# Attention and feed-forward on one Trainium2 core: three tiles of the normalised x turned by DMA instead of by TensorE

## The chip, the core and the metric

The kernel runs on 1 core of one Trainium2 chip. The time is device microseconds (us) of one execution; where several executions are given, the median stands. The profile is one execution taken by the hardware profiler. PE is TensorE (PEld its weight loads), ACT is ScalarE, DVE is VectorE, POOL is GpSimd and SP is SyncE, which here only issues DMAs.

## The reference

```python
def _attn_ref(q, k, v, g_norm):                 # q, k, v: 8 batches, 8 heads, 576 rows, 64
    kv = np.einsum('bhsd,bhse->bhde', k, v)
    out = np.einsum('bhsd,bhde->bhse', q, kv)
    rms = np.sqrt(np.mean(out * out, axis=-1, keepdims=True) + 1e-06)
    return (out / rms * g_norm)
def _moe_ref(x, g_ln, w_ch1, w_ch2):            # x: 8, 576, 512
    mu = np.mean(x, axis=-1, keepdims=True)
    var = np.mean((x - mu) ** 2, axis=-1, keepdims=True)
    xn = (x - mu) / np.sqrt(var + 1e-06) * g_ln
    ch = np.maximum(xn @ w_ch1, 0.0) @ w_ch2    # 512 -> 2048 -> 512
    return (x + ch)
```

The attention has no softmax: k and v of a batch make one 64x64 matrix for each head, and q is multiplied with it. Its output, normalised for each head, is the x of a feed-forward part with a layer norm in front.

## The kernel before

The 8 x 576 rows of x are cut into 36 tiles of 128 rows, numbered in the order in which they are worked on; tiles 0 to 8 are of batches 0 and 1, tiles 9 to 17 of batches 2 and 3, and so on, and the last of each nine holds 64 rows of both batches. Four tiles make a block. Batch 3 begins with tile 13.

A tile's way is in `plan_tile` (L738): the attention matmul (`t_out`, L444), the squares on ACT (L457), their sums on DVE (L466), the root on ACT (L470), x on DVE (L492 or L496), its mean, and the centred and scaled `xc` in bf16 (`t_xc`, L518, three buffers). The feed-forward needs `xc` with its features in the partitions, so each tile's 128x512 is turned into `xT`, a buffer for a block. This is done in one of two ways:

- on TensorE (`t_turn_pe`, L525): four 128x128 transposes into PSUM, and a copy to `xT` on ACT (`t_turn_out`, L532);
- by DMA (`t_turn_dma`, L536): one `dma_start_transpose` on SP's queue straight from `xc` to `xT`.

The condition at L785, `n < N_PE_TURN` with 12, picks the first for tiles 0 to 11 and the second for tiles 12 to 35.

The first matmul of the feed-forward (`m1`) runs tile by tile for blocks 0 and 1 (L575) and for a whole block of four tiles from block 2, that is tiles 8 to 11, on (L590). The second (`m2`) is L609. Its result is scaled and added to x on DVE (L616) and stored from SP (L622).

The k, v and q of a batch are loaded by POOL's queue (L232, L239, L247), permuted by copies on ACT (L373), and q of batches 2 to 7 is then turned by one large DMA transpose on SP's queue into `qT` (L413); k and v make the head matrices in L421. For batches 3 to 7 POOL first waits in `gate` (L683) until the xT of a certain tile is there: tiles 5, 6 and 7 for batch 3's k, q and v, and tiles 11, 12 and 13 for batch 4's.

Nothing is scheduled by a compiler. All pieces are declared as steps with an engine, an assumed cost, a key of priority and their dependencies, and `run_plan` (L104) puts them in order: it takes the step that can start first by its assumed costs, and among equals on one engine the one with the lowest key. The DMAs go through one assumed server, one after the other. The copies of k and q of batch 3 wait in the plan for 6 us behind the planned landing of their load (`x.lag`, L716). Each engine then works through its list strictly in that order, and real waits are on semaphores. A DMA turn of a tile is planned with an occupancy of 1.235 us on SP and 0.5 us in the server; a PE turn with 0.23 us on PE and a copy of a PSUM tile on ACT.

Of the kernel before, what the change touches and what calls it, by code (L numbers as in the profile page):

```python
# [14 lines left out]
def kernel(  # L15
# [27 lines left out]
    N_TILES = B * S // 128  # L43
    N_BLK = N_TILES // 4
    FINE = (0, 1)
    N_PE_TURN = 12
    N_SUM = 12
    LOOK = 8
    XB = 18
# [44 lines left out]
    def add(eng, occ, dur, key, deps, fn, dma=None, alloc=None, main=False, lag=0.0):  # L94
        s = Step()
        s.eng, s.occ, s.dur, s.key, s.fn = eng, occ, dur, key, fn
        s.deps = [d for d in deps if d is not None]
        s.dma, s.alloc, s.main, s.frees, s.behind = dma, alloc, main, None, None
        s.start = s.done = None
        s.lag = lag  # L100
        steps.append(s)
        return s
# [335 lines left out]
    def t_out(n, h0=0, h1=H):  # L438
        bs, t = TILES[n]
        ps = psum.tile([128, H, D], f32, tag="out", name="out_ps", bufs=BANKS["out"])  # L440
        o3 = ps.rearrange("p h e -> p (h e)").rearrange("p (hp he) -> p hp he", hp=HP)
        for hp in range(h0 // 2, h1 // 2):
            for i, b in enumerate(bs):
                nc.tensor.matmul(  # L444
                    o3[:, hp, :], lhsT=att[b]["qT"][:, 4 * t + hp, :],
                    rhs=kv_pack[b % 3][:, hp, :],
                    start=(i == 0), stop=(i == len(bs) - 1))
        st[n]["ps", h0] = ps
# [6 lines left out]
    def t_sq(n, h0=0, h1=H):  # L455
        sq = buf(n, "sq", [128, H, D], h0)
        nc.scalar.activation(sq[:, h0:h1, :], st[n]["ps", h0][:, h0:h1, :], func=AF.Square)  # L457

    def t_xg(n, h0=0, h1=H):
        xg = buf(n, "xg", [128, H, D], h0)  # L460
        nc.vector.tensor_mul(xg[:, h0:h1, :], st[n]["ps", h0][:, h0:h1, :],  # L461
                             gn.to_broadcast([128, h1 - h0, D]))

    def t_red(n, h0=0, h1=H):
        ss = buf(n, "ss", [128, H, 1], h0)
        nc.vector.tensor_reduce(ss[:, h0:h1, :], st[n]["sq"][:, h0:h1, :], axis=AX.X, op=ALU.add)  # L466

    def t_rms(n, h0=0, h1=H):
        rms = buf(n, "rms", [128, H, 1], h0)
        nc.scalar.activation(rms[:, h0:h1, :], st[n]["ss"][:, h0:h1, :], func=AF.Sqrt,  # L470
                             scale=1.0 / D, bias=eps_attn)

    def t_inv(n, h0=0, h1=H):
        inv = buf(n, "inv", [128, H, 1], h0)
        nc.vector.reciprocal(inv[:, h0:h1, :], st[n]["rms"][:, h0:h1, :])
# [9 lines left out]
    def t_x(n, h0=0, h1=H):  # L485
        m, i = divmod(n, 4)
        block_tiles(m)
        x = buf(n, "x", [128, H, D], h0, XB)
        inv = st[n]["inv"][:, h0:h1, :].to_broadcast([128, h1 - h0, D])
        if n < N_SUM:  # L490
            sums = blk[m]["sums"][:, i, 0:1] if h1 == H else blk[m]["half"]
            nc.vector.tensor_tensor_reduce(  # L492
                out=x[:, h0:h1, :], in0=st[n]["xg"][:, h0:h1, :], in1=inv, scale=1.0, scalar=0.0,
                op0=ALU.mult, op1=ALU.add, accum_out=sums)
        else:
            nc.vector.tensor_mul(x, st[n]["xg"], inv)  # L496
        if h1 == H:
            st[n]["x"] = x.rearrange("p h d -> p (h d)")

    def t_mean(n):  # L500
        m, i = divmod(n, 4)
        if n < N_SUM:
            if n in HALVED:
                nc.vector.tensor_scalar(
                    blk[m]["mv"][:, i, 0:1], blk[m]["sums"][:, i, 0:1], blk[m]["half"], 1.0 / Dm,
                    op0=ALU.add, op1=ALU.mult)
            else:
                nc.vector.tensor_scalar_mul(
                    blk[m]["mv"][:, i, 0:1], blk[m]["sums"][:, i, 0:1], 1.0 / Dm)
        else:  # L510
            stats = work.tile([128, 6], f32, tag="stats", name="stats")
            nc.vector.bn_stats(stats, st[n]["x"])  # L512
            nc.vector.bn_aggr(blk[m]["mv"][:, i, :], stats)
# [15 lines left out]
    def t_turn_out(n, f0=0, f1=Dm):  # L529
        m, i = divmod(n, 4)  # L530
        kk = slice(f0 // 128, f1 // 128)
        nc.scalar.copy(blk[m]["xT"][:, kk, i * 128:(i + 1) * 128], st[n]["tps", f0][:, kk, :])  # L532
# [205 lines left out]
    def plan_tile(n):  # L738
        bs, t = TILES[n]
        m, i = divmod(n, 4)  # L740
        p = pos[n]
        dn = done[n]
        deps = []
        for b in bs:
            deps += adone[b]["kv"] + adone[b]["qT", t]
        if n >= 12:
            deps.append(main_at(okey[n] - EARLY))
        def cost(c, h0, h1):
            return c((h1 - h0) * D)
        halves = ((0, H // 2), (H // 2, H)) if n in HALVED else ((0, H),)  # L750

        q0 = okey[n] if n // 4 not in FINE else p - 12
        xs = []
        for h0, h1 in halves:
            hh = dict(h0=h0, h1=h1)
            w = (h1 - h0) / H
            d = [adone[0]["kv"][h0 // 4], adone[0]["qT", 0][h0 // 4]] if n in HALVED else deps
            o = add("PE", 0.23 * len(bs) * w, 0.23 * len(bs) * w + 0.2, okey[n], d,
                    lambda hh=hh: t_out(n, **hh), alloc="out")
            sq = add("ACT", *cost(act_cost, h0, h1), q0 + 4,  # L760
                     [o] + [done[n - 3]["red"] if n >= 3 else None], lambda hh=hh: t_sq(n, **hh))
            red = add("DVE", 0.6 * w, 0.6 * w + 0.08, q0 + 5, [sq], lambda hh=hh: t_red(n, **hh))
            o.frees = xg = add("DVE", *cost(dve_cost, h0, h1), q0 + 5.5, [sq, gn_done],
                               lambda hh=hh: t_xg(n, **hh))
            rms = add("ACT", 0.2, 0.3, q0 + 5.8, [red], lambda hh=hh: t_rms(n, **hh))
            inv = add("DVE", 0.12, 0.2, q0 + 6.5, [rms], lambda hh=hh: t_inv(n, **hh))
            xdeps = [inv, xg]
            if n >= XB:
                xdeps.append(done[n - XB]["store"])
            extra = 0.08 if n < N_SUM else 0  # L770
            occ, dur = cost(dve_cost, h0, h1)
            xs.append(add("DVE", occ + extra, dur + extra, q0 + 7, xdeps, lambda hh=hh: t_x(n, **hh)))
        for b in bs:
            adone[b].setdefault("outs", []).append(o)
        dn["red"] = red
        few = n < N_SUM
        mean = add("DVE", 0.15 if few else 0.8, 0.2 if few else 0.9, q0 + 7.5, xs, lambda: t_mean(n))
        m1_before = blk[m - 3]["m1done"] if m >= 3 else None
        turned = []
        for h0, h1 in halves:  # L780
            ff = dict(f0=h0 * D, f1=h1 * D)
            w = (h1 - h0) / H
            xc = add("DVE", 0.6 * w + 0.06, 0.6 * w + 0.15, q0 + 8, [mean, load["gl"][0]],
                     lambda ff=ff: t_xc(n, **ff))
            if n < N_PE_TURN:  # L785
                tp = add("PE", 0.23 * w, 0.23 * w + 0.22, q0 + 9, [xc, ident, m1_before],
                         lambda ff=ff: t_turn_pe(n, **ff), alloc="kvt")
                tp.frees = add("ACT", *cost(act_cost, h0, h1), q0 + 10, [tp],
                               lambda ff=ff: t_turn_out(n, **ff))
                turned.append(tp.frees)  # L790
            else:
                turned.append(add_dma("SP", q0 + 9, [xc, m1_before], lambda: t_turn_dma(n),
                              0.5e3, 1.0, occ=1.235, lat=0.25, tail=0.42))
        dn["xT"] = turned
        var = [mean]
        if few:
            var.append(add("ACT", 0.68, 0.83, p + 5, xs + dn["xT"], lambda: t_s2(n)))
        blk[m].setdefault("var", []).extend(var)
        if m in FINE or i == 3:
            vd = var if m in FINE else blk[m]["var"]  # L800
            e = last_pos[n if m in FINE else 4 * m] - 6
            if few:
                vd = [add("DVE", 0.2, 0.3, e, vd, lambda: b_var(n))]
            s = add("ACT", 0.2, 0.3, e + 1, vd, lambda: b_std(n))
            r = add("DVE", 0.12, 0.2, e + 2, [s], lambda: b_rstd(n))
            for j in ((n,) if m in FINE else range(4 * m, 4 * m + 4)):
                done[j]["rstd"] = r
# [4 lines left out]
    def main_at(i):  # L812
        return mains_made[i] if 0 <= i < len(mains_made) else None
# [125 lines left out]
```

## Time and profile before

| what | value |
|---|---|
| time, median of 5 runs | 297.55 us (296.88 to 297.65) |
| the profiled execution's own time | 297.24 us |
| its span, first to last instruction | 295.5 us |
| granted TensorE clock | 1.000 |
| L525, PE transposes of xc | x48, 4.7 us busy |
| L532, copies of them on ACT | x13, 0.58 us each for a full tile |
| L536, DMA transposes of xc | x24, median 2.6 us from issue to landing, 2.4 to 9.4 |
| L413, DMA transposes of q | x6, median 5.9 us, 4.9 to 7.7 |

How to read the lines that follow. A row of the timeline is: start in us from the span's start, us, engine, line, operation, what is written and read, the number of instructions merged in the row, and in brackets the idle time before it with what ended it. A row of the chain is: start, us, and what ended last there. A row of the DMA issues ends with the median of us from issue to landing; asked for a window with one issue in it, that is this issue's own time. The DMA share of a stretch is the time of all packets over 16 engines' time; it passes 1 where an engine has more than one packet in flight.

### The profile page before, as it was taken

The page shows a single profiled execution, that of the slowest core. Times are in us where ns is not written, and L with a number is a line of the kernel's source. Part 1 is how long each engine was busy: PE and PEld are TensorE (multiplying, and loading weights), DVE is VectorE, ACT ScalarE, POOL GpSimd, SP SyncE. Part 2 cuts the span into 40 slices and gives each one's busy share as a digit, 9 for nine tenths or more (in the row PEclk, how much of TensorE's full clock was granted, in tenths as well). Part 3 has the DMA queues.
Part 4 walks back from the last instruction along what each step waited for, and adds up shares of the span by engine and source line. Part 5 has one row for each costly group of instructions (what it writes and reads, how often), then busy time and mean ns, then how long its engine had stood idle before and what let it go on. Part 6 is the DMA issues. An engine that isn't in the chain of part 4 may idle for free.

```text
span 295.5 us, 5131 instructions
## 1 busy us (share of the span) xinstructions
PE 281.8 (95%) x2017; PEld 160.8 (54%) x2045; DVE 165.8 (56%) x359; ACT 160.0 (54%) x308; POOL 53.5 (18%) x88
## 2 busy tenths in 40 slices
PE   3979999999999999999999999999999999999994
PEld 1869955877754445444544445544554444444443
DVE  1597048759695778556754875577557755320022
ACT  3268972987977842783269417841761176016400
POOL 8873230205120402300222020210000000000000
PEclk9999999999999999999999999999999999999999
DMA  6999999648979699996478949895101310220012
GB/s 97 182 199 205 203 199 191 167 91 108 193 137 135 86 177 189 121 167 133 116 121 100 184 130 128 100 158 154 55 18 53 91 53 19 61 96 4 0 73 71
DMA packets 75932, 35.21 MB, mean 119 GB/s; under 512 B 44547, under 2 KB 71427, under 8 KB 75908
## 3 DMA queue, kind: packets, MB, share of 16 engines
q0 software_dynamic: 41888, 18.35, 51.1%
q1 hardware_dynamic: 33860, 16.39, 23.4%
q8 instruction: 16, 0.26, 0.3%
q10 hardware_dynamic: 160, 0.13, 0.2%
q14 instruction: 8, 0.07, 0.1%
HBM read 36.70 MB, written 9.44 MB: 156 GB/s over the span
## 4 chain that ended last, share of the span: by engine, by line
PE 87%; DMA 10%; issue 1%; POOL 1%; DVE 0%; POOLq 0%
PE mm_ps L609 41%; PE mm_ps L590 31%; PE mm_ps L575 8%; DMA w<-in_moe_w_ch_dram 5%; PE out_ps L444 3%; DMA qT<-qp 3%; DMA vb<-in_v_dram 3%; PE kv_ps L421 2%; PE xT_ps L525 1%; POOL kb L232 1%; PE qT_ps L393 0%; POOL vb L232 0%; DVE x L616 0%; POOL qp L253 0%; POOLq L923 0%
## 5 line engine op out<-in xcount | busy, mean ns | idle before, releaser
L609 PE MATMUL mm_ps<-w,m 128*128 128x512 bf16 (+1 forms) x577 | 129.3, 373 | 0.7
L590 PE MATMUL mm_ps<-xT,w 128*128 128x512 bf16 x435 | 99.6, 379 | 0.6
L597 ACT ACTIVATE m<-mm_ps 128x512 bf16<-128x512 f32 x112 | 66.1, 597 | 43.8 <-PE mm_ps L590 42.8
L609 PEld LDWEIGHTS <-m 128*128 128x128 bf16 x592 | 56.7, 98 | 59.8
L590 PEld LDWEIGHTS <-w 128*128 128x128 bf16 x448 | 43.1, 98 | 48.6
L466 DVE TENSOR_REDUCE ss<-sq 128x8 f32<-128x512 f32 (+1 forms) x37 | 24.8, 669 | 47.1 <-ACT sq L457 46.9
L616 DVE SCALAR_TENSOR_TENSOR x<-mm_ps,rstd,x 128x512 f32<-128x512 f32 (+1 forms) x37 | 27.0, 733 | 40.0 <-PE mm_ps L609 39.9
L457 ACT ACTIVATE sq<-out_ps 128x512 f32<-128x512 f32 (+1 forms) x37 | 21.5, 584 | 47.9 <-PE out_ps L444 47.9
L575 PE MATMUL mm_ps<-xT,w 128*128 128x128 bf16 x512 | 30.9, 219 | 1.0 <-ACT xT L532 0.7
L575 PEld LDWEIGHTS <-w 128*128 128x128 bf16 x512 | 29.3, 98 | 2.0 <-issue 0.8
L518 DVE SCALAR_TENSOR_TENSOR xc<-x,mv,gl 128x512 bf16<-128x512 f32 (+1 forms) x37 | 27.1, 737 | 1.2
L461 DVE TENSOR_TENSOR xg<-out_ps,gn 128x512 f32<-128x512 f32 (+1 forms) x37 | 24.7, 668 | 0.3
L683 POOL COPY mark<-xT 128x1 bf16<-128x1 bf16 x15 | 3.8, 252 | 98.5 <-DMA xT<-xc 83.1
L582 ACT ACTIVATE m<-mm_ps 128x512 bf16<-128x512 f32 x32 | 18.3, 597 | 3.1 <-PE mm_ps L575 2.4
L496 DVE TENSOR_TENSOR x<-xg,inv 128x512 f32<-128x512 f32 x24 | 16.6, 691 | 0.8
L512 DVE BATCH_NORM_STATS2 stats<-x 128x6 f32<-128x512 f32 x24 | 16.5, 689 | 0.5
L444 PEld LDWEIGHTS <-qT 128*128 128x128 bf16 x160 | 11.5, 98 | 8.1 <-DMA qT<-qp 1.1
L470 ACT ACTIVATE rms<-ss,eps_attn 128x8 f32<-128x8 f32 (+1 forms) x37 | 11.1, 300 | 8.6 <-DVE ss L466 8.6
L444 PE MATMUL out_ps<-kv_pack,qT 128*128 128x128 bf16 x160 | 15.0, 220 | 0.8 <-DMA qT<-qp 0.6
L373 ACT COPY kp<-kb 128x1024 bf16<-128x1024 bf16 (+1 forms) x14 | 15.2, 1101 | 0.0
L421 PE MATMUL kv_ps<-vb,kp 128*128 128x128 bf16 (+1 forms) x144 | 11.4, 230 | 3.3 <-DMA vb<-in_v_dram 3.3
L436 DVE CAST kv_pack<-kv_ps 64x256 bf16<-64x256 f32 (+1 forms) x18 | 7.1, 392 | 13.4 <-PE kv_ps L421 13.3
(59 smaller groups left out, 169.6 us busy)
## 6 DMA issues: line engine op xcount, KB each, us to landing
out_dram<-x SPq DMA_DIRECT2D x32, 256.0 KB, 2.9
w<-in_moe_w_ch_dram POOLq DMA_DIRECT2D x8, 512.0 KB, 13.3
qb<-in_q_dram POOLq DMA_DIRECT2D x7, 512.0 KB, 6.3
kb<-in_k_dram POOLq DMA_DIRECT2D x6, 512.0 KB, 8.5
vb<-in_v_dram POOLq DMA_DIRECT2D x6, 512.0 KB, 8.7
out_dram<-x SPq DMA_DIRECT2D x6, 128.0 KB, 2.4
qp<-in_q_dram POOLq DMA_DIRECT2D x10, 64.0 KB, 6.1
kb<-in_k_dram POOLq DMA_DIRECT2D x2, 288.0 KB, 5.5
```

The source lines that it names most:

```text
L421: nc.tensor.matmul(ps[:, hp, :], lhsT=kp[b % 2][p, t, 2 * hp:2 * hp + 2, :].rearrange("p h d -> p (h d)"), rhs=(v5[b % 2][:, 2 * hp:2 * hp ...
L444: nc.tensor.matmul(o3[:, hp, :], lhsT=att[b]["qT"][:, 4 * t + hp, :], rhs=kv_pack[b % 3][:, hp, :], start=(i == 0), stop=(i == len(bs) - 1))
L457: nc.scalar.activation(sq[:, h0:h1, :], st[n]["ps", h0][:, h0:h1, :], func=AF.Square)
L461: nc.vector.tensor_mul(xg[:, h0:h1, :], st[n]["ps", h0][:, h0:h1, :], gn.to_broadcast([128, h1 - h0, D]))
L466: nc.vector.tensor_reduce(ss[:, h0:h1, :], st[n]["sq"][:, h0:h1, :], axis=AX.X, op=ALU.add)
L518: nc.vector.scalar_tensor_tensor(xc[:, f0:f1], in0=st[n]["x"][:, f0:f1], scalar=blk[m]["mv"][:, i, 0:1], in1=gl[:, f0:f1], op0=ALU.subtrac ...
L575: nc.tensor.matmul(ps[:, d, :], lhsT=w1[c][:, kk, d * 128:(d + 1) * 128], rhs=blk[m]["xT"][:, kk, i * 128:(i + 1) * 128], start=(kk == 0), ...
L582: nc.scalar.activation(st[n]["m1"][:, c, :, :], st[n]["m1ps", c], func=AF.Relu)
L590: nc.tensor.matmul(ps, lhsT=w1[c][:, kk, d * 128:(d + 1) * 128], rhs=blk[m]["xT"][:, kk, :], start=(kk == 0), stop=(kk == nKm - 1))
L597: nc.scalar.activation(blk[m]["m1", c][:, d, :], blk[m]["m1ps", g], func=AF.Relu)
L609: nc.tensor.matmul(st[n]["m2ps", f0], lhsT=m1_piece(n, c, d), rhs=w2[c][:, d, f0:f1], start=(c == 0 and d == 0), stop=(c == 3 and d == 3))
L616: nc.vector.scalar_tensor_tensor(x[:, f0:f1], in0=st[n]["m2ps", f0], scalar=blk[m]["rstd"][:, i, :], in1=x[:, f0:f1], op0=ALU.mult, op1=AL ...
```

## The change

Tiles 8, 9 and 10 are turned by DMA on SP's queue; tiles 0 to 7 and tile 11 stay on TensorE. The steps of these three tiles, and what depends on them, are declared anew in the same place, with the assumed costs that the two kinds had before, and the plan is made from them.

```diff
-    N_PE_TURN = 12
+    PE_TURN = (0, 1, 2, 3, 4, 5, 6, 7, 11)
...
-            if n < N_PE_TURN:
+            if n in PE_TURN:
                 tp = add("PE", 0.23 * w, 0.23 * w + 0.22, q0 + 9, [xc, ident, m1_before],
                          lambda ff=ff: t_turn_pe(n, **ff), alloc="kvt")
                 tp.frees = add("ACT", *cost(act_cost, h0, h1), q0 + 10, [tp],
                                lambda ff=ff: t_turn_out(n, **ff))
                 turned.append(tp.frees)
             else:
                 turned.append(add_dma("SP", q0 + 9, [xc, m1_before], lambda: t_turn_dma(n),
                               0.5e3, 1.0, occ=1.235, lat=0.25, tail=0.42))
```

## The prediction

> **What bounds the kernel now.** I read the head of the page first, then the chain that ended last between 82 and 93 us, then the timelines of TensorE, VectorE and GpSimd around tiles 8 to 11, and last the DMA issues with their time to landing.
>
> ```profile
> span 295.5 us, 5131 instructions
> ...
> PE 281.8 (95%) x2017; PEld 160.8 (54%) x2045; DVE 165.8 (56%) x359; ACT 160.0 (54%) x308; POOL 53.5 (18%) x88
> ```
>
> TensorE is busy for 281.8 of 295.5 us, and the whole-kernel groups put only 0.6 to 1.0 us of idle time before each of its large lines (L609, L590, L575, L444). From the first tile on the kernel is one unbroken queue of matmuls, so a change is worth what it takes out of that queue, less the idle time that it puts in. The chain around the edit:
>
> ```profile
> 81.89 1.94 PE mm_ps L609 x9
> 83.83 0.23 PE xT_ps L525 x4
> 84.06 7.68 DMA qT<-qp
> 91.74 0.05 issue
> 91.78 0.40 PE out_ps L444 x4
> ```
>
> The reader is to see two things: what a tile's four transposes cost in the queue (0.23 us here, 0.22 in the chain's other rows of L525), and one place where TensorE does stand still: the attention of batch 3 at 91.78 waits for the DMA transpose of q, for 0.57 us by the timeline.
>
> **Removed.** Three tiles by four PE transposes, 3 x 0.22 = 0.66 us of TensorE's queue. They stand at 71.85 (tile 8, the second half of that row), 76.03 and 79.77; the row at 83.67 is tile 11 and stays:
>
> ```profile
> 71.85 0.61 PE L525 MATMUL xT_ps<-identity,xc 128*128 128x128 bf16 x8
> ...
> 76.03 0.39 PE L525 MATMUL xT_ps<-identity,xc 128*128 128x128 bf16 x4
> ...
> 79.77 0.39 PE L525 MATMUL xT_ps<-identity,xc 128*128 128x128 bf16 x4
> ...
> 83.67 0.39 PE L525 MATMUL xT_ps<-identity,xc 128*128 128x128 bf16 x4
> ...
> 85.62 1.03 PE L590 MATMUL mm_ps<-xT,w 128*128 128x512 bf16 x4
> ```
>
> The 0.39 us is the length of four alone, overlapped with neighbours at both ends; the next instruction's start moves by the chain's 0.22, so I take that. ScalarE loses three copies of 0.58 us (L532), 1.7 us where it is busy for 3.76 of 4.00 us (74 to 78) and 4.89 of 5.00 us (78 to 83). Nothing on TensorE stands still there, so I cost this relief at nothing for TensorE. It can bring forward the statistics of tile 11 and the copies of q. The planner, though, holds the k and q copies back by a fixed lag of 6 us behind their loads, so I do not count on that.
>
> A rule of the Trainium skill speaks against the edit. "VectorE: DVE Perf Modes", section "The three transpose paths", gives 390 ns for a 128x128 bf16 transpose on TensorE and 1309 ns by DMA, and its rules advise TensorE where PSUM will do as the destination. By 390 ns each the twelve removed would be worth an estimated 4.7 us. The rows above show four of them taking 0.22 us, so the trace decides for 0.66.
>
> **Added.** Three DMA transposes on SP's queue, as L536 does for tiles 12 to 35: 1.2 us of issue each, and nobody else needs SP at that time (its rows are a store at 67.39, a store at 75.00, a store at 83.55, the q transpose at 84.06). The centred x of tiles 8, 9 and 10 is ready at 69.5, 72.8 and 76.8 by VectorE's rows, so they issue there. A store stuck behind them is needed by nobody before its x buffer comes round 18 tiles later. VectorE has three xc buffers: tile 11's xc (82.11) must now wait until tile 8's transpose has landed, tile 12's (87.43) until tile 9's. Tile 8 has 12.6 us from issue, tile 9 14.6; the longest landing on record is 9.4, so I cost that at nothing.
>
> The disputed cost is when they land. Three loads are in flight on GpSimd's queue, and a transpose lands very differently with and without such company. Tile 12's landed after 9.4 us, issued at 88.21 behind a load at 85.82; tile 13's, with no load about:
>
> ```profile
> xT<-xc SPq DMA_TRANSPOSE x1, 9.4
> ```
> ```profile
> xT<-xc SPq DMA_TRANSPOSE x1, 2.4
> ```
>
> The loads around the edit:
>
> ```profile
> 66.96 0.88 POOL L232 DMA_DIRECT2D kb<-in_k_dram  x1 [0.23 <-issue]
> ...
> 68.81 0.88 POOL L239 DMA_DIRECT2D qb<-in_q_dram  x1
> ...
> 73.44 0.88 POOL L232 DMA_DIRECT2D vb<-in_v_dram  x1 [0.27 <-issue]
> 74.31 0.69 POOL L247 DMA_DIRECT2D v<-in_v_dram  x1
> ```
>
> By the DMA issues these land at 75.7 (k), 78.8 (q, 10.0 us), 82.8 and 83.1 (the two parts of v, 9.3 and 8.8 us). Transposes issued within 2.5 us of a load's issue took 8.8 to 9.4 us (tiles 12, 14, 16: issues at 88.21, 101.13, 113.36) and landed within 0.25 us of that load's last part. Tile 15's, issued 5.1 us after the last load, took 4.6. Tile 10's would go at 76.8, 2.5 us after the last part of v, so between the two. Bounds: 76.8 + 2.4 = 79.2 and 76.8 + 9.4 = 86.2. I take "it lands with v". A transpose alone fills the DMA engines for 0.55 x 1.2 = 0.66 us (217.5 to 218.7, where only it moves), and the engines are full between 74 and 78 (share 1.54: more than one packet in flight on each), so three push v's end from 83.1 to at most 85.1. TensorE wants the block-2 x at 85.62 - 0.66 = 84.96 and v for L421 at 86.48 - 0.66 = 85.82. At the upper bound the wait is 0.1 us: I cost it at nothing, with no reserve.
>
> A rule of "DMA: Bandwidth & Descriptors", section "Rules for kernel authors", says that a transpose next to ordinary DMAs needs nothing. It is about right data; read as a rule on time it would let tile 10 land at 79.2 with everything covered. The landings of 8.8 to 9.4 us beside loads speak against that reading, so I do not lean on it.
>
> **The sum.** The 0.57 us wait for q stays as it is if the q copies (81.83 on ScalarE), the issue at 84.06 and the load that slows it (k of batch 4, released by tile 11's copy) all move forward with TensorE. Then the profiled execution's 297.24 us (span 295.5) becomes 297.24 - 0.66 = 296.58. That execution lies 0.31 under the median of the runs, 297.55, so the median becomes 296.89, and I say **296.9**. About 0.2% (0.6 us) is what a measurement of this kernel can tell from no change, so even the whole gain would barely clear it.
>
> **Rivals.**
> *The q wait shrinks too* (faster). ScalarE's relief brings the q copies forward by up to the two 0.58 us copies that precede them after 76, so q's transpose lands earlier against TensorE and the 0.57 us go as well: 297.55 - 0.66 - 0.57 = 296.3. For it: ScalarE is full there. Against it: the planner's lag, and ScalarE's work that waits for TensorE in between.
> *The gain is given back at 91.78* (no change). The q transpose lands at 91.74 whatever comes before, because its own transfer of 7.7 us is slowed by other traffic (others took 4.9 to 6.5) and now queues behind tile 10's. TensorE arrives 0.66 us sooner and waits 0.57 + 0.66 = 1.23 us: 297.55. For it: it is the one wait on the chain. Against it: the planner may put another matmul group ahead of the attention.
> *The transposes land behind the loads* (slower). Place: the first matmul of block 2. If tile 10's takes the 9.4 us of tile 12's, it lands at 86.2, and TensorE waits 86.2 - 84.96 = 1.3 us with everything queued behind it: 297.55 - 0.66 + 1.3 = 298.2. It decides against the change once the landing takes over 8.1 + 0.7 = 8.8 us. The same traffic also slows the loads: k of batch 5 and its small part took 8.3 and 10.2 us beside tile 16's transpose, against 6.3 and 5.8 for batch 6. With 1.3 us more at the waits for v or q it is 299.1 (a load's 4.4 us longer, less the cover that it has). For it: three transposes rather than one enter a full queue, and there is no reserve. Against it: tile 10's is issued when v is already well under way.
> That the edit does not do what it says I exclude: the condition at L785 alone picks the path.
>
> **How the numbers follow.** Forecast 42% (296.5 to 297.3, about two thirds of it past the 0.2%), q wait gone too 12%, gain given back 12%, slower 34%. Faster: 0.28 + 0.12 = 0.40; within 0.2%: 0.14 + 0.12 = 0.26; slower: 0.34. The range reaches from the faster rival less 0.2 us, 296.1, to the slower rival's end, 299.1; the likeliest case alone spans 296.5 to 297.3.
>
> **What will show it.** Right: 36 PE transposes in L525 instead of 48, 27 in L536 instead of 24; L590's first matmul about 0.7 us earlier with no idle time before it that names xT's DMA; the attention of batch 3 waiting about 0.6 us for qT. The slower rival: an idle TensorE before L590 or L421 around 85, with DMA xT<-xc or v named, and v landing past 85. Given back: the qT wait at about 1.2 us. The forecast also fails if the planner, which prices a DMA transpose at about a microsecond, reorders TensorE's queue so that some other wait opens up.

## The result and the profile after

The changed kernel is slower: a median of 299.41 us (54 runs) beside 298.36 us (94 runs) for the kernel before, a ratio of 1.0041 with a 95% interval of 1.0029 to 1.0054, that is 1.2 us. The forecast of 296.9 had the wrong sign and its range ended at 299.1. It started from 297.55, the median of five runs; with 298.36 for the kernel before, 0.8 us of the distance between 296.9 and 299.41 has nothing to do with the change.

The profiled execution of the changed kernel took 300.25 us. The head of its page, with the granted TensorE clock in 40 slices:

```profile
span 298.5 us, 5115 instructions
...
PE 283.1 (95%) x2005; PEld 160.6 (54%) x2033; DVE 165.6 (55%) x359; ACT 158.6 (53%) x305; POOL 53.7 (18%) x88
...
PEclk9999999999998999999999999999999999999999
```

The twelve matmul instructions are gone (2017 to 2005) and so are three on ACT (308 to 305), as planned; the span is 3.0 us longer, and one slice shows less than the full clock. The answer of the waits, of which only the lines that grew or are new are copied (total us, times, longest):

```profile
POOL mark L683 <- ACT rms L470: 12.0, 1, 12.0
...
ACT rms L470 <- DVE ss L466: 10.1, 14, 2.3
...
DVE xc L518 <- DMA xT<-xc: 3.1, 1, 3.1
...
PE out_ps L444 <- DMA qT<-qp: 2.1, 1, 2.1
...
PE mm_ps L590 <- ACT xT L532: 1.3, 1, 1.3
```

The third line is the new one: VectorE stands still for 3.05 us in front of an xc, waiting for a DMA transpose. The last two are TensorE's; the first of them was 0.57 us, the other was not there. The chain between 60 and 100 us ties them together:

```profile
68.62 9.42 DMA xT<-xc
...
78.14 0.75 DVE xc L518
...
79.15 0.61 DVE ss L466
...
79.98 1.97 ACT kp L373 x2
...
83.25 1.88 ACT qp L373 x2
85.13 0.07 ACT xT L532
85.20 8.07 DMA qT<-qp
93.27 0.05 issue
93.32 0.40 PE out_ps L444 x4
```

Read from the top: tile 8's transpose, issued at 68.62, lands at 78.04. VectorE's xc at 78.14 is tile 10's, and it waited for that landing. Behind it in VectorE's list stands the sum of squares of tile 11 (L466), for which ScalarE waits in front of tile 11's root (2.27 us); in the new order that root stands ahead of the copies of k, where before it stood behind them. ScalarE's timeline before:

```profile
78.74 1.98 ACT L373 COPY kp<-kb 128x1024 bf16<-128x1024 bf16 x2
80.62 0.30 ACT L470 ACTIVATE rms<-ss,eps_attn 128x8 f32<-128x8 f32 x1
```

So the copies of k (79.98, before 78.74), those of q (83.15, before 81.83) and tile 11's xT (85.03, before 84.09) are all late, and with the q copies the q transpose: 85.20 in place of 84.06. TensorE pays in two places, shown by its timeline:

```profile
82.22 0.40 PE L525 MATMUL xT_ps<-identity,xc 128*128 128x128 bf16 x4
...
85.66 2.53 PE L590 MATMUL mm_ps<-xT,w 128*128 128x512 bf16 x11 [1.32 <-ACT xT L532]
...
93.32 0.40 PE L444 MATMUL out_ps<-kv_pack,qT 128*128 128x128 bf16 x4 [2.06 <-DMA qT<-qp]
```

In the profiled execution a third cost follows. In the busy times by stretch (PE, PEld, DVE, ACT, POOL, then the granted clock, DMA share, GB/s):

```profile
95.00:96.00 1.00, 1.00 (x4) 0.42 (x3) 0.94 (x4) 0.57 (x2) 0.00 (x0) 0.50 1.46 138
96.00:97.00 1.00, 1.00 (x7) 0.58 (x5) 0.97 (x2) 0.51 (x2) 0.19 (x1) 0.50 0.02 1
```

The clock is at half for 3.41 us (94.3 to 97.7), which costs 1.7 us. The ledger of the two profiled executions, by the starts of the same matmul groups: the changed kernel is 0.89 us ahead at 60 us, before any of this (at the start it waited less for its loads), and 3.21 us behind from 105 us to the end. The 4.1 us between are -0.67 for the transposes, +0.12 in front of tile 11's own turn, +1.48 in front of L590, +1.50 more in front of L444 and +1.67 of clock. (By the starts L590 loses 0.16 us more than the idle time in its row, which counts from the end of the matmul before; the next one otherwise starts 0.16 us before that end.) The half clock is not in every run: of 53 runs, one slow run left out, 9 have a mean clock under 0.9955, with a median of 300.95 us, and the 38 at 0.9985 or more have 299.31. The kernel before, in the 64 runs beside the experiments that have such a clock, has 297.89. So the 1.2 us are mostly the waits.

### The profile page after: what moved, and what is told of

Same layout as the page of the kernel before. It is cut to its first block, busy times and chain, and to the rows that moved or that the text cites. A ratio compares the mean times of both kernels' runs of the same rounds, so it can differ in the third digit from the quotient of the medians.

```text
span 298.5 us, 5115 instructions
## 1 busy us (share of the span) xinstructions
PE 283.1 (95%) x2005; PEld 160.6 (54%) x2033; DVE 165.6 (55%) x359; ACT 158.6 (53%) x305; POOL 53.7 (18%) x88
## 4 chain that ended last, share of the span: by engine, by line
PE 80%; DMA 13%; ACT 3%; DVE 1%; issue 1%; POOL 1%; DVEq 0%; POOLq 0%
PE mm_ps L609 37%; PE mm_ps L590 30%; PE mm_ps L575 7%; DMA w<-in_moe_w_ch_dram 4%; DMA xT<-xc 3%; PE out_ps L444 3%; DMA qT<-qp 3%; DMA vb<-in_v_dram 3%; PE kv_ps L421 2%; ACT kp L373 1%; ACT m L597 1%; ACT qp L373 1%; POOL kb L232 0%; PE qT_ps L393 0%; ACT sq L457 0%
## 5 line engine op out<-in xcount | busy, mean ns | idle before, releaser
L590 PE MATMUL mm_ps<-xT,w 128*128 128x512 bf16 x436 | 101.2, 383 | 1.8 <-ACT xT L532 1.3
L590 PEld LDWEIGHTS <-w 128*128 128x128 bf16 x448 | 43.5, 99 | 50.9 <-issue 3.0
L466 DVE TENSOR_REDUCE ss<-sq 128x8 f32<-128x512 f32 (+1 forms) x37 | 24.8, 669 | 48.5 <-ACT sq L457 48.3
L518 DVE SCALAR_TENSOR_TENSOR xc<-x,mv,gl 128x512 bf16<-128x512 f32 (+1 forms) x37 | 27.1, 736 | 4.2 <-DMA xT<-xc 3.1
L444 PE MATMUL out_ps<-kv_pack,qT 128*128 128x128 bf16 x160 | 15.3, 223 | 2.4 <-DMA qT<-qp 2.1
L444 PEld LDWEIGHTS <-qT 128*128 128x128 bf16 x160 | 11.7, 99 | 10.0 <-DMA qT<-qp 2.6
L470 ACT ACTIVATE rms<-ss,eps_attn 128x8 f32<-128x8 f32 (+1 forms) x37 | 11.1, 299 | 10.2 <-DVE ss L466 10.1
```

Source lines behind the costliest of these rows:

```text
L444: nc.tensor.matmul(o3[:, hp, :], lhsT=att[b]["qT"][:, 4 * t + hp, :], rhs=kv_pack[b % 3][:, hp, :], start=(i == 0), stop=(i == len(bs) - 1))
L518: nc.vector.scalar_tensor_tensor(xc[:, f0:f1], in0=st[n]["x"][:, f0:f1], scalar=blk[m]["mv"][:, i, 0:1], in1=gl[:, f0:f1], op0=ALU.subtrac ...
L590: nc.tensor.matmul(ps, lhsT=w1[c][:, kk, d * 128:(d + 1) * 128], rhs=blk[m]["xT"][:, kk, :], start=(kk == 0), stop=(kk == nKm - 1))
```

## The experiments

Theory 1 was the buffer: tile 10's xc is given the buffer that tile 8's DMA has not yet read. Theory 2 was the traffic: three more transposes slow the loads and the q transpose, whatever the buffers. All ratios are to the kernel before on the same chip; the runs are spread over four chips, on which the kernel before had medians of 297.94, 297.95, 298.13 and 298.36 us, so differences of medians between chips are good to a few tenths at best.

**Five xc buffers in the changed kernel.** Every engine's order of work is unchanged.

```diff
-        xc = buf(n, "xc", [128, Dm], f0, 3, bf16)
+        xc = buf(n, "xc", [128, Dm], f0, 5, bf16)
```

> The changed kernel with five xc buffers in place of three; nothing else differs, every engine's order of work is the same. Theory 1 (the buffer): VectorE's wait of 3.05 us in front of tile 10's xc for tile 8's landing is what made the change slow, by way of ScalarE; with it go the 1.32 us in front of L590 and the extra 1.49 us in front of the attention of batch 3, and what is left is the gain of 0.66 us: a ratio to before of 0.998 (0.996 to 0.999). Theory 2 (the traffic): the three transposes slow the loads and the q transpose whatever the buffers are: the ratio stays at 1.004 and the wait in front of the attention at 2 us.

Measured: 297.86 us, 0.9985 (0.9955 to 1.0016). The wait at L518 is gone. Two of TensorE's remain, the second as large as with three buffers:

```profile
PE out_ps L444 <- DMA qT<-qp: 2.0, 1, 2.0
...
PE mm_ps L590 <- DMA xT<-xc: 0.7, 1, 0.7
```

So the loss goes with the buffer, but the whole forecast gain is not there: tile 10's transpose took 8.92 us from 76.35 and landed at 85.27, for which TensorE waited 0.73 us, and the q transpose took 9.6 us.

**Five xc buffers in the kernel before**, the same edit.

> The kernel before with five xc buffers, the control. Both theories: no difference, ratio 1.000 (0.998 to 1.002), since nothing waits for an xc buffer before tile 12.

Measured: 298.24 us, 1.0027 (0.9996 to 1.0057): no difference that the interval separates. Its profile held something else: the q transpose took 8.9 us and TensorE waited 1.8 us for it, in a kernel without the change. The wait that I had read as 0.57 us swings from one execution to the next.

**The traffic alone.** The kernel before with five xc buffers and three more transposes that nobody reads; to make room, x has 17 buffers in place of 18 and a scratch tile of ScalarE one.

```diff
+                if n in (8, 9, 10):        # beside TensorE's own turn
+                    add_dma("SP", q0 + 9.5, [xc], lambda: t_turn_spare(n),
+                            0.5e3, 1.0, occ=1.235, lat=0.25, tail=0.42)
+    spare = [consts.tile([128, nKm, 128], bf16, name=f"spare{i}") for i in range(3)]
+    def t_turn_spare(n):
+        nc.sync.dma_start_transpose(spare[n - 8], st[n]["xc"])
```

> The kernel before, TensorE turning tiles 8 to 10 as ever, and beside it the same three DMA transposes at the same time into spare buffers that nobody reads, with five xc buffers so that nobody waits for them. It does more than the computation needs and isolates the traffic. Theory 1: no difference, ratio 1.000 to 1.002. Theory 2: the loss of the change plus the 0.66 us that are not gained here, (1.2 + 0.66) us, ratio 1.006.

Measured: 298.48 us, 1.0021 (0.9989 to 1.0053). Theory 2's 1.006 is outside the interval, theory 1's 1.000 inside; its profile had a wait for q of 2.97 us and 0.82 us for v. I do not count it as decided, because of that swing.

**Tile 8 alone, and tile 9 alone, by DMA.**

```diff
-    PE_TURN = (0, 1, 2, 3, 4, 5, 6, 7, 11)
+    PE_TURN = (0, 1, 2, 3, 4, 5, 6, 7, 9, 10, 11)   # 8 alone; for 9 alone 8 in place of 9
```

> Tile 8 alone by DMA; 9, 10 and 11 on TensorE; three xc buffers. Theory 1: tile 10's xc still waits for tile 8's landing, so nearly the whole loss is there with a third of the gain: ratio 1.003 to 1.005, with a wait of some 3 us at L518. Theory 2: a third of the traffic, ratio 1.001 to 1.002.

> Tile 9 alone by DMA; 8, 10 and 11 on TensorE; three xc buffers. One DMA transpose among the same loads as in the run with tile 8 alone, but the xc that takes over its buffer is tile 12's at 87, 15 us after the issue. Theory 1 (the buffer): no wait at L518, a ratio of 0.999 to 1.001. Theory 2 (the traffic): as with tile 8 alone, 1.006 or more.

Measured: tile 8 alone 300.86 us, 1.0091 (1.0059 to 1.0123); tile 9 alone 297.72 us, 0.9992 (0.9962 to 1.0023). One transpose among such loads costs 2.7 us or nothing, depending on which tile is given its buffer next. A part of the 2.7 is clock: the five of its nine runs with a mean clock of 0.9985 or more have a median of 299.38, 1.5 us over the kernel before at that clock on the same chip (297.86). VectorE's, ScalarE's and TensorE's timelines with tile 8 alone:

```profile
78.39 0.75 DVE L518 SCALAR_TENSOR_TENSOR xc<-x,mv,gl 128x512 bf16<-128x512 f32 x1 [2.89 <-DMA xT<-xc]
```
```profile
79.50 0.29 ACT L560 ACTIVATE std<-mv,eps_ln 128x1 f32<-128x1 f32 x1 [2.25 <-DVE mv L553]
...
80.18 1.98 ACT L373 COPY kp<-kb 128x1024 bf16<-128x1024 bf16 x2
```
```profile
84.36 0.40 PE L525 MATMUL xT_ps<-identity,xc 128*128 128x128 bf16 x4 [1.09 <-DVE xc L518]
```

TensorE, which now turns tiles 10 and 11 itself, meets the late xc directly (1.09 us), beside 2.02 us for q, and this profile too has 3.4 us of half clock. Here the root of tile 11 stands behind the copies of k, as in the kernel before, and ScalarE is held up all the same, by tile 7's standard deviation (L560): it stands ahead of them, and its input stands behind tile 10's xc in VectorE's list. Whether one tile by DMA is really worse than three is open: at a clock of 0.9985 or more the changed kernel has 299.31. I had put it at 1.003 to 1.005, too low. With tile 9 alone there is no wait at L518 at all.

**A hold that takes the swing away.** GpSimd issues batch 4's k load only when batch 3's q transpose has landed; TensorE's order is unchanged.

```diff
-                if b == 3:
+                if b in (3, 4):
                     pool_do(0.1, lambda: nc.gpsimd.tensor_copy(
-                        mark, att[2]["qT"][:, 0, 0:1]), [adone[2]["qfree"]])
+                        mark, att[b - 1]["qT"][:, 0, 0:1]), [adone[b - 1]["qfree"]])
```

> The kernel before, and GpSimd issues batch 4's k load only when batch 3's q transpose has landed; TensorE's order is the same. The control for the next run. The q transpose should land about 5 us after its issue (at 89) in place of 7.7 to 8.9, so the wait in front of batch 3's attention (0.57 us in the profile of before, 1.8 in that of before with five buffers) goes: 0.6 to 1.8 us faster, ratio 0.994 to 0.998. If the q transpose is slow for another reason than that load, 1.000.

> The changed kernel with five xc buffers and the same hold on batch 4's k load. Theory 1: with five buffers alone TensorE still waited 0.73 us for tile 10's xT and 2.03 us for q; the second goes here, so 0.66 us of transposes and up to 0.57 us of the old q wait are gained against before, less 0.7 for tile 10: ratio 0.996 to 0.999, level with the control or a little better. Theory 2: the transposes' traffic still holds up v and q, ratio 1.001 or more, and slower than the control.

> As the run before it, but tile 10 goes back to TensorE, which takes the one wait for xT away that five buffers left: 0.44 us of transposes gained and the q wait gone, ratio 0.994 to 0.997, the best of the four if theory 1 holds. By theory 2 it stands between the control and the run with three tiles.

Measured: the kernel before with the hold 296.10 us, 0.9931 (0.9905 to 0.9957); with three tiles by DMA and five buffers 295.94, 0.9925 (0.9901 to 0.9949); with tiles 8 and 9 by DMA 295.32, 0.9903 (0.9857 to 0.9948), the fastest kernel of this study. The DMA issue of q in the kernel before with the hold:

```profile
qT<-qp SPq DMA_TRANSPOSE x1, 5.0
```

It was 7.7 us without the hold, 8.9 with five buffers, and no wait for q is left on TensorE. All nine runs lie between 295.67 and 296.48 us, where the kernel before on the same chip ranged from 296.82 to 302.51. So that collision was most of the kernel's spread and about 2 us of its median, and with the hold kernels on one chip can be told apart to a few tenths. Three tiles gain almost nothing on the control (0.16 us) since TensorE waits 0.8 us for tile 10's xT; with tile 10 back on TensorE no such wait is left and the gain is 0.78 us, somewhat more than the 0.44 us of transposes.

**The change and the traffic again, under the hold.** The first is the changed kernel with three buffers as the pool hands them out; the second the spare transposes.

> The changed kernel as it is, three xc buffers, with the hold on batch 4's k load; every engine's order of work is that of the run with five buffers and the hold, so the two differ in the buffer alone, and the wait for q, which swings most from run to run, is out of the way in both. Theory 1 (the buffer): VectorE waits some 3 us at tile 10's xc and TensorE 1.3 us in front of L590 in place of 0.8: 0.5 to 1 us slower than with five buffers (295.94), so 296.4 to 297.0, ratio 0.995 to 0.997, and slower than the control with the hold (296.10). Theory 2 (the traffic): as with five buffers, 295.9.

> The run with three transposes into spare buffers beside TensorE's own, now with the hold on batch 4's k load: the traffic alone, more work than the computation needs, without the swing of the wait for q. Theory 1: what the traffic costs by itself is the wait for v, 0.55 + 0.27 us in the run without the hold: 296.1 + 0.8 = 296.9 at most, ratio 0.993 to 0.996. Theory 2: 296.1 + 1.9 = 298, ratio 0.999 or more.

Measured: 297.08 us, 0.9965 (0.9942 to 0.9988), and 295.68 us, 0.9904 (0.9875 to 0.9933). The waits of the first:

```profile
DVE xc L518 <- DMA xT<-xc: 3.8, 1, 3.8
...
PE mm_ps L590 <- ACT xT L532: 1.3, 1, 1.3
...
PE xT_ps L525 <- DVE xc L518: 0.7, 1, 0.7
```

With the same order of work on every engine and the same loads and transposes, the buffer alone makes 297.08 - 295.94 = 1.1 us. The two stood on different chips (the ratios differ by 0.4%, with intervals that just overlap), but TensorE's waits agree: 0.73 + 1.32 = 2.05 us here, 0.78 us with five buffers. The traffic alone shows no cost: 295.68 is not slower than the control's 296.10, also on another chip, and on one chip the changed kernel is 1.4 us slower than the kernel with the spare transposes, though TensorE has less to do in it. The stretches of that run show that the traffic was there (DMA share 1.52 in the second, where before had 1.03):

```profile
74.00:78.00 4.00, 4.00 (x70) 3.87 (x69) 3.85 (x12) 3.64 (x9) 0.64 (x1) 1.00 1.55 148
78.00:83.00 5.00, 4.95 (x30) 2.50 (x29) 2.31 (x6) 5.00 (x8) 0.00 (x0) 1.00 1.52 178
```

Theory 2, which wanted 298 or more, falls as the cause of the loss. Why this run is 0.4 us faster than the control is open; its list on TensorE has batch 3's kv matmuls one group later.

**Three buffers, handed out strictly in turn.** Each tile names its buffer; `buf` takes the name as a new argument.

```diff
-        xc = buf(n, "xc", [128, Dm], f0, 3, bf16)
+        xc = buf(n, "xc", [128, Dm], f0, 1, bf16, f"xc{n % 3}")
```

> The changed kernel with its three xc buffers handed out strictly in turn (tile n takes n mod 3), so that tile 10 takes over tile 7's and tile 11 tile 8's; the same memory, and the same order of work on every engine. Theory 1, made sharper (the wait is there because tile 10 is given tile 8's buffer, before its DMA has read it): no wait at tile 10's xc and at most a few tenths at tile 11's, as with five buffers: ratio 0.997 to 1.000. If three buffers are simply too few, the wait moves to tile 11 and the ratio stays at 1.003 or more.

> The same with the hold on batch 4's k load, to be read beside 297.08 us (three buffers as the pool gives them) and 295.94 (five). Theory 1, sharper: 295.7 to 296.3, ratio 0.991 to 0.994. Too few buffers: 296.8 to 297.3.

Measured: 297.57 us, 0.9996 (0.9970 to 1.0021), and with the hold 296.29 us, 0.9938 (0.9917 to 0.9958), beside 297.08 with the pool's order (on another chip). VectorE's timeline of the run with the hold, tiles 10 and 11:

```profile
75.04 0.75 DVE L518 SCALAR_TENSOR_TENSOR xc<-x,mv,gl 128x512 bf16<-128x512 f32 x1
...
79.39 0.75 DVE L518 SCALAR_TENSOR_TENSOR xc<-x,mv,gl 128x512 bf16<-128x512 f32 x1 [0.63 <-DMA xT<-xc]
```

Tile 10 does not wait, tile 11 waits 0.63 us. With the same memory and the same order of work the loss is gone: what made the change slow is which buffer tile 10 was given. But no gain is left either: in the run with the hold TensorE still waits in front of L590, now for tile 10's own transpose, which took 9.5 us.

```profile
PE mm_ps L590 <- DMA xT<-xc: 1.3, 1, 1.3
```

## Why the prediction was wrong, step by step

**"Tile 11's xc (82.11) must now wait until tile 8's transpose has landed ... I cost that at nothing": this step failed.** The wait was seen and the landing bounded (9.4 us; it took 9.42), but the wrong tile was put behind it. The pool does not always hand its three buffers out in turn: in these programs the next taker gets the one whose last reader comes first in the program. In the kernel before that is the turn, and tile 10's xc has the address of tile 7's. In the changed kernel tile 8's reader, the DMA, is issued right behind its xc, and tile 7's, the PE transposes, stands later in the program, so that tile 10's xc has the address of tile 8's, as it has with tile 8 alone; with tile 9 alone it has tile 7's again. So tile 10 was given tile 8's buffer, wanted it at 75.1 and had it at 78.04. The price that the text gave itself, "tile 8 has 12.6 us from issue", was for tile 11; for tile 10 it is 75.1 - 68.6 = 6.5 us, under the 8.8 to 9.4 us beside it. Even in turn the 12.6 us would not have held: there tile 11 wanted its xc at 78.8, some 10.2 us after tile 8's issue, and waited in one run of the two. Nor did I look up what stands behind that xc in VectorE's list, and who waits for it: ScalarE's root of tile 11, and behind it everything that TensorE then waited for.

**"ScalarE's relief ... at nothing for TensorE"**: the relief did not help. In the new plan tile 11's root stands ahead of the k copies, and by it VectorE's wait became ScalarE's; that the relief is why it moved was not tested. The loss does not depend on it: with tile 8 alone the root had not moved, and the wait came through L560.

**Removed, 0.66 us**: right in size. The same attention matmul starts at 80.86 before and 79.30 after the change, when three tiles are past: the lead has grown from 0.89 to 1.56 us, by 0.67.

**"It lands with v", no wait**: nearly right. With five buffers tile 10's landed at 85.27 and cost 0.73 us; the last part of v came at 85.6 in the changed kernel and at 86.3 with five buffers, later than the 85.1 that was my upper bound.

**"The 0.57 us wait for q stays as it is"**: wrong twice. In the changed kernel the q copies were late, and the wait is not a constant: 0.57 and 1.8 us in two profiles of kernels without the change, 2.0 in the changed one with five buffers. Nor was the start of the sum a constant: the profile and the five runs that it stands on were on the fast side of a spread of 6 us.

**The rivals.** The one on the slower side named the right place, the first matmul of block 2, and, by luck, the right price (1.3 us), but the wrong mechanism: TensorE waited there for ScalarE's copy of tile 11, the one tile of the block that was not moved. Its upper end was added up wrongly: 298.2 and 1.3 us more are 299.5, not 299.1. The gain that is given back at 91.78 happened too, and more than given back: the wait there became 2.06 us, not 1.23, and mostly by the late q copies (1.14 us), not by a queue behind tile 10. The share of 34% for slower was too small for an edit with no reserve anywhere.

## What to carry to other kernels

Where a reader of a shared buffer moves to a slower path, ask which tile is given that buffer next (by the program's addresses or waits, not by counting in turn), and what is queued behind that tile's writer. The cost of such a wait is read off the lists of the engines behind it, here VectorE, then ScalarE, then TensorE. And before a change of half a microsecond is tried, take out the wait that swings by more: here one more condition on a load was worth 0.7% and made the other differences visible.

## What the runs showed of the hardware

The q transpose took 4.9 to 6.4 us in the six profiles with the hold, and 7.7 to 10.0 us in the eight without, where a 512 KB load was issued 0.6 to 1.8 us after it: in these profiles a transfer is slowed by what is issued after it. In the changed kernel's profile TensorE's clock was granted at half for 3.41 us after waits of 1.32 and 2.06 us, and with tile 8 alone after waits of 1.09 and 2.02 us; with five buffers waits of 0.73 and 2.03 us were followed by none, nor was a wait of 2.97 us in the run with the spare transposes. What decides it these runs do not show.
